# Exponentials of the memory slots brought to token order through a DRAM scratch instead of TensorE turnings

## The chip, the core and the metric

The kernel runs on one core of a Trainium2 chip. The metric is the device time of one execution in microseconds. Engines are named as in the profile: PE is TensorE (matmuls; PEld its weight loads), DVE is VectorE, ACT is ScalarE, POOL is GpSimd, SP is SyncE, whose queue issues most DMAs.

## The reference

An attention over 32 learned memory slots feeds a mixture of experts with one expert per token. All in float32.

```python
# attention: batch 8, heads 8, tokens S = 576, head size D = 64, slots M = 32
a = exp(phi - max over tokens); a = a / (sum over tokens + 1e-9)
k_m = einsum('bhsm,bhsd->bhmd', a, k); v_m = einsum('bhsm,bhsd->bhmd', a, v)
attn = softmax(q @ k_m^T / 8); x = attn @ v_m          # 576 tokens of 512 per batch
# experts: 8, hidden 1024
logits = normed(x) @ normed(expert_emb).T / tau; e = argmax(logits)
out = softmax(logits)[e] * (relu(x @ w1[e]) @ w2[e])
```

The part that the change touches is the first line: exp(phi - max), and the sums over tokens that use it as a weight.

## The kernel before

The eight batches run one after the other in a pipeline of three. While batch b goes through its expert, the attention of batch b + 1 (the object u in the code) is finished and its expert chosen, and the slots of batch m = b + 2 are made. The program is written out by hand in the order of each engine: every engine takes its instructions in that order. TensorE's work sets the steps. The first layer of a batch has 16 steps (first[0] to first[15]: two halves of 288 tokens by eight blocks of the hidden size, six matmuls each, L629); the second layer has 40 (second[0] to second[39]: the tail of 64 tokens in eight steps, L671, then tiles 0 to 3 of 128 tokens in eight steps each of three matmuls, L682). Each float32 product is made from three matmuls of split operands: the split of W2 into wh and wl is made by GpSimd (L599, L600), that of the hidden layer by ScalarE (hh, L632) and VectorE (hl, L635). The function steps() hangs the rest of the work on these steps.

The slots of a batch come as follows. load_phi reads phi, laid out with (4 heads x 32 slots) on the partitions and 576 tokens along a row, for two groups g of heads, into ex. largest (L413) takes the maximum over tokens on VectorE into nm, softmax (L428) the exponential on ScalarE, in place in ex. The sums over tokens are matmuls with tokens on the partitions, so ex has to be turned: turn (L450) makes nine 128 x 128 transposes on TensorE into te, and ScalarE copies them to eT (L451). slots (L470) multiplies eT with the keys and values kx and kl; blocks scales the result; flip turns it once more for the later steps. In a batch b of 1 or more, softmax of m stands at second[11] and second[14], turn at second[28], with the load of the next phi behind it, and slots at second[31], with load_kv of the next batch behind it. In batch 0 these stand at 18, 21, 32 and 35.

The attention of batch b + 1: its scores come out as sT, with heads and slots on the partitions; u.fill (L63) turns them by VectorE's 32 x 32 block transpose into x, with tokens on the partitions; there they are weighed and divided. u.lay (L99) writes x in 128-byte pieces to a DRAM scratch td, and three reads (L103, L105) bring it back to ea in token order. u.attend (L115) makes the rows po; VectorE reduces them to lg, the maximum m and the flags oh (L120, L122, L123); choose counts the tokens of each expert on TensorE (L156) and takes the largest to seli. SP reads seli, and issues the loads of W1 (w1s) and W2 (w2s) and two writes to DRAM (keep: ad and vd). In batch 0, whose steps lie later, fill is at second[3] and second[7], lay at second[7] and second[10], attend at second[24], [26] and [28], choose at second[29].

SP issues its DMAs in the order of the program; there are eight completion semaphores in turn, so each DMA also waits until the one eight places before it has landed. PSUM has four buffers m0 to m3 for sums (tag m) and four for the rest (tag t).

Of the kernel before, what the change touches and what calls it, by code (L numbers as in the profile page):

```python
# [8 lines left out]
F32 = mybir.dt.float32  # L9
# [10 lines left out]
P = 128  # L20
B, H, S, D, M = 8, 8, 576, 64, 32
N, DM, E, FF = B * S, H * D, 8, 1024
NG = 2
# [208 lines left out]
class Kernel:  # L232
# [4 lines left out]
    def __init__(self, ctx, tc, phiT, qT, kv, kvt, emb, tau, w1, w2, out):  # L237
        self.tc, self.nc = tc, tc.nc
        self.phiT, self.qT, self.kv, self.kvt, self.emb, self.tau = phiT, qT, kv, kvt, emb, tau
        self.w1 = w1.rearrange("e p (c f) -> e p c f", c=NC)  # L240
        self.w2 = w2.rearrange("e p (c f) -> e p c f", c=8)
        self.out = out
        self.st = ctx.enter_context(tc.tile_pool(name="st", bufs=1))
        self.wk = ctx.enter_context(tc.tile_pool(name="wk", bufs=2))
        self.ps = ctx.enter_context(tc.tile_pool(name="ps", bufs=1, space=PSUM))
        dp = ctx.enter_context(tc.tile_pool(name="dram", bufs=1, space=DRAM))
        st = self.st.tile
        self.ad = dp.tile([B, P, NG, S], F32, name="ad")
        self.vd = dp.tile([B, P, NC * D], F32, name="vd")
        self.td = dp.tile([B, S, NG, 4, 32], F32, name="td")  # L250

        self.ex = st([P, NG * S + 64], F32, name="ex")
        self.kx = [st([P, H, 2 * D], F32, name=f"kx{k}") for k in range(4)]
        self.kl = st([P, 4, 2 * D], F32, name="kl")
        self.qt = st([P, NC, S], F32, name="qt")
        self.eT = st([P, 9, P], F32, name="eT")
        self.kvb = st([P, 2, NG, 4, D], F32, name="kvb")
        self.kb, self.vb = self.kvb[:, 0], self.kvb[:, 1]
        self.kT = st([P, NC, D], F32, name="kT")
        self.sT = st([P, NG, S], F32, name="sT")  # L260

        self.vT = [st([P, NG, 2, D + 2 * E], F32, name=f"vT{i}") for i in range(2)]

        self.vv = st([P, NG, P + E], F32, name="vv")

        self.x = st([P, NG, BL, 32], F32, name="x")
        self.ea = st([P, NT, NG * P], F32, name="ea")
        self.rs, self.known = {}, set()
        self.aT = [st([P, NG, S], F32R, name=f"aT{k}") for k in range(2)]
        self.aw = st([P, NG, S2], F32, name="aw")  # L270

        self.w1s = st([P, NC, FF], F32, name="w1s")
        self.w2s = st([P, 8, DM], F32, name="w2s")
        self.wh = st([P, 8, DM], F32R, name="wh")
        self.wl = st([P, 8, DM], F32R, name="wl")
        self.gh = st([P, NG, FF], F32R, name="gh")
        self.gl = st([P, NG, FF], F32R, name="gl")
        self.hh = st([P, 8, S], F32R, name="hh")
        self.hl = st([P, 8, S], F32R, name="hl")
        self.h4 = st([P, 8, 64], F32, name="h4")  # L280

        self.gate = st([P, B, NT], F32, name="gate")
        self.idx = st([P, B, NT], F32, name="idx")
        self.fl = st([P, B, E], F32, name="fl")
        self.seli = st([1, B], I32, name="seli")
        self.halves = self.turns = 0
        self.tags, self.sums = 3, 0
# [72 lines left out]
    def load_phi(self, b, gs=range(NG)):  # L360
        if b < B:
            for g in gs:
                to = self.e(b, g)
                if g and b > 1:
                    self.nc.sync.dma_start(to[:, 64:], self.phiT[b, :, g, : 4 * P])
                    self.nc.sync.dma_start(to[:, :64], self.phiT[b, :, g, 4 * P :])
                else:
                    self.nc.sync.dma_start(to, self.phiT[b, :, g])

    def load_kv(self, b):  # L370
        if b < B:
# [38 lines left out]
        return self.rs[b]  # L410

    def largest(self, b, g):
        self.nc.vector.tensor_reduce(  # L413
            out=self.room(b)[0][:, g : g + 1], in_=self.e(b, g), axis=AX.X, op=ALU.max, negate=True
        )
        self.known.add((b, g))
# [28 lines left out]
    def turn(self, b, i0, i1):  # L445
        t = self.pt([P, 4, P], f"te{b}_{i0}")
        for i in range(i0, i1):
            g, k = divmod(i, 4)
            o = 5 * P * g + P * k if i < 8 else 4 * P
            self.nc.tensor.transpose(t[:, i - i0], self.ex[:, o : o + P], self.ident)  # L450
        self.nc.scalar.copy(self.eT[:, i0:i1], t[:, : i1 - i0])  # L451
        if i1 == 9 and b > 1:
            self.load_phi(b + 1)

    def slots(self, b, accs=None, gs=range(NG), ks=range(5), first=True, last=True):

        nc = self.nc
        if first:
            self.accs = accs or [self.pt([P, 2 * D], f"acc{b}_{g}") for g in range(NG)]
        accs = self.accs  # L460

        def to(i, g):
            r = slice(32 * i, 32 * i + 32)
            return accs[g][r, i] if len(accs[g].shape) == 3 else accs[g][r]

        def add(g, j, k):
            r = slice(64 * g, 64 * g + 64) if k == 4 else slice(P)
            e = self.eT[r, 4 * g + k if k < 4 else 8, 32 * j : 32 * j + 32]
            x = self.kl[r, j] if k == 4 else self.kx[k][:, 4 * g + j]
            nc.tensor.matmul(  # L470
                to(j ^ g, g), lhsT=e, rhs=x, start=first and k == ks[0], stop=last and k == ks[-1]
            )

        for g in gs:
            for k in ks:
                for j in range(4 if k < 4 else 0):
                    add(g, j, k)
        for j in range(4 if 4 in ks else 0):
            for g in gs:
                add(g, j, 4)  # L480
        if b > 1:
            self.load_kv(b + 1)

    def block(self, b, g, which=(0, 1), alone=False):

# [205 lines left out]
    def steps(self, b, t, u):  # L691


        first, second = ([[] for _ in range(n)] for n in (16, 40))
# [13 lines left out]
        if u:  # L708
            c, o = b + 1, 0 if b else 3
# [16 lines left out]
            o = 0 if b else 7  # L726
# [10 lines left out]
            second[32 + o].append(lambda: list(after))  # L737
            m = b + 2
            if m < B:
                for g in range(NG):  # L740
                    second[11 + 3 * g + o].append(lambda g=g: self.softmax(m, (g,)))
                second[18 + o].append(lambda: self.shares(m))
                second[(28 if b else 25) + o].append(lambda: [self.turn(m, i, min(i + 4, 9)) for i in (0, 4, 8)])
                at = second[(31 if b else 28) + o]
                at += [lambda: self.slots(m), lambda: self.blocks(m, 0), lambda: self.blocks(m, 1, True)]
                for g in range(NG):
                    second[(35 + 2 * g if b else 31 + g) + o].append(lambda g=g: self.flip(m, g))
# [281 lines left out]
```

## Time and profile before

| | us |
|---|---|
| median of 3 runs | 418.94 (418.16 to 420.54) |
| the profiled execution, its time | 419.85 |
| its span in the trace | 418.1 |
| PE busy | 404.8 |
| DVE busy | 262.0 |
| ACT busy | 169.6 |
| POOL busy | 173.0 |

The time of an execution holds the span and what lies around it. Batch 0's second layer begins at 49.5 us and batch 1's project step at 82.9 us; from batch 3 on a batch takes some 48.6 us. In the groups of the trace, a row has the line, the engine, the operation, out<-in by the program's names and the number of instructions. In the timeline a row has the start, the length, the engine and its line; what stands in brackets is the idle time of the engine before it and what ended that. Rows with SPq are the issues of DMAs, not their transfers. A row of windows has the stretch, its length, the busy time of PE, PEld, DVE, ACT and POOL with their instructions, the granted clock of TensorE (PEclk), the share of the 16 DMA engines and GB/s.

### The profile page before, as it was taken

The page shows a single profiled execution, that of the slowest core. Times are in us where ns is not written, and L with a number is a line of the kernel's source. Part 1 is how long each engine was busy: PE and PEld are TensorE (multiplying, and loading weights), DVE is VectorE, ACT ScalarE, POOL GpSimd, SP SyncE. Part 2 cuts the span into 40 slices and gives each one's busy share as a digit, 9 for nine tenths or more (in the row PEclk, how much of TensorE's full clock was granted, in tenths as well). Part 3 has the DMA queues.
Part 4 walks back from the last instruction along what each step waited for, and adds up shares of the span by engine and source line. Part 5 has one row for each costly group of instructions (what it writes and reads, how often), then busy time and mean ns, then how long its engine had stood idle before and what let it go on. Part 6 is the DMA issues. An engine that isn't in the chain of part 4 may idle for free. (4 is left out here: it accounts for less than half of the span.)

```text
span 418.1 us, 9433 instructions
## 1 busy us (share of the span) xinstructions
PE 404.8 (97%) x3491; PEld 328.7 (79%) x3491; DVE 262.0 (63%) x839; ACT 169.6 (41%) x468; POOL 173.0 (41%) x205
## 2 busy tenths in 40 slices
PE   7889999999999999999999999999999999999993
PEld 3458878788887978879887988879788888879783
DVE  5597894679664795549772795647955495745000
ACT  4475521465225722356313742347213661145110
POOL 0035671297032932168130960339331681359000
PEclk9999999999999999999999999999999999999997
DMA  8989934996679835994469916797349405690101
GB/s 266 348 308 375 364 72 117 313 362 251 153 229 396 320 57 126 361 368 192 76 216 390 386 53 143 253 380 314 63 132 355 159 0 98 204 402 2 38 36 47
DMA packets 69858, 91.19 MB, mean 218 GB/s; under 512 B 41800, under 2 KB 47688, under 8 KB 69808
## 3 DMA queue, kind: packets, MB, share of 16 engines
q1 hardware_dynamic: 66928, 82.00, 59.0%
q0 software_dynamic: 2688, 8.26, 5.3%
q8 instruction: 29, 0.48, 0.5%
q10 hardware_dynamic: 192, 0.28, 0.2%
q14 instruction: 21, 0.17, 0.1%
HBM read 71.19 MB, written 19.33 MB: 217 GB/s over the span
## 5 line engine op out<-in xcount | busy, mean ns | idle before, releaser
L629 PE MATMUL ph<-aT,gh 128*128 128x288 f32 x512 | 103.3, 297 | 0.5 <-DVE gl L613 0.5
L682 PE MATMUL py<-wh,hh 128*128 128x512 f32 x248 | 102.4, 413 | 0.0
L682 PE MATMUL py<-wl,hh 128*128 128x512 f32 x248 | 97.0, 391 | 0.3 <-POOL wl L600 0.3
L682 PE MATMUL py<-wh,hl 128*128 128x512 f32 x248 | 97.1, 392 | 0.0
L600 POOL TENSOR_TENSOR wl<-w2s,wh 128x512 fp32r<-128x512 f32 x64 | 83.9, 1311 | 5.2
L629 PEld LDWEIGHTS ph<-aT,gh 128*128 128x128 f32 x512 | 81.6, 188 | 3.1 <-DVE gl L613 1.4
L629 PE MATMUL ph<-aT,gl 128*128 128x288 f32 x256 | 75.3, 294 | 0.0
L635 DVE SCALAR_TENSOR_TENSOR hl<-ph,hh 128x288 fp32r<-128x288 f32 x128 | 56.1, 450 | 21.0 <-ACT hh L632 15.7
L687 ACT ACTIVATE ys<-py,gate 128x512 f32<-128x512 f32 (+1 forms) x39 | 25.1, 643 | 103.5 <-PE py L682 55.0
L632 ACT ACTIVATE hh<-ph 128x288 fp32r<-128x288 f32 x128 | 52.2, 416 | 32.6 <-PE ph L629 32.0
L793 POOL DMA_DIRECT2D out_dram<-ys x28 | 15.5, 553 | 117.3 <-ACT ys L687 109.6
L682 PEld LDWEIGHTS py<-wh,hh 128*128 128x128 f32 x248 | 46.6, 188 | 12.0 <-issue 4.3
L682 PEld LDWEIGHTS py<-wh,hl 128*128 128x128 f32 x248 | 46.5, 188 | 10.2
L682 PEld LDWEIGHTS py<-wl,hh 128*128 128x128 f32 x248 | 46.7, 188 | 8.5 <-POOL wl L600 0.7
L629 PEld LDWEIGHTS ph<-aT,gl 128*128 128x128 f32 x256 | 48.0, 188 | 0.0
L590 POOL TENSOR_TENSOR aT<-aw,aT 128x576 fp32r<-128x576 f32 (+3 forms) x20 | 23.7, 1205 | 47.0 <-PE py L682 33.8
L599 POOL CAST wh<-w2s 128x512 fp32r<-128x512 f32 x64 | 42.4, 663 | 0.7 <-DMA w2s<-w 0.6
L613 DVE TENSOR_TENSOR gl<-pg,gh 128x512 fp32r<-128x512 f32 x32 | 19.9, 683 | 34.8 <-ACT gh L612 34.8
L671 PE MATMUL py<-w2s,h 128*64 128x256 f32 x256 | 29.4, 382 | 0.0
L120 DVE TENSOR_REDUCE lg<-po 128x8 f32<-128x16 f32 x40 | 6.9, 174 | 31.7 <-PE po L115 30.4
L671 PEld LDWEIGHTS py<-w2s,h 128*64 128x64 f32 x256 | 17.7, 137 | 9.4 <-DVE hl L635 1.0
L115 PEld LDWEIGHTS po<-vv,aw 128*128 128x128 f32 x160 | 21.8, 189 | 3.2 <-ACT kT L517 1.0
(168 smaller groups left out, 506.7 us busy)
## 6 DMA issues: line engine op xcount, KB each, us to landing
kx<-kv SPq DMA_DIRECT2D x32, 512.0 KB, 7.1
w2s<-w SPq DMA_DIRECT2D x32, 512.0 KB, 10.7
w1s<-w SPq DMA_DIRECT2D x28, 512.0 KB, 6.6
out_dram<-ys POOLq DMA_DIRECT2D x28, 256.0 KB, 6.0
qt<-qT SPq DMA_DIRECT2D x12, 576.0 KB, 8.1
ad<-aw SPq DMA_DIRECT2D x8, 576.0 KB, 12.8
td<-x SPq DMA_DIRECT2D x56, 72.0 KB, 2.2
ea<-td SPq DMA_DIRECT2D x7, 512.0 KB, 4.2
```

The source lines that it names most:

```text
L115: nc.tensor.matmul(po[:, 144 * g : 144 * g + P + E], lhsT=k.aw[:, g, to], rhs=k.vv[:, g], start=True, stop=True)
L590: self.nc.gpsimd.tensor_tensor(out=al, in0=a, in1=ah.bitcast(F32), op=ALU.subtract)
L599: (copy or self.nc.scalar.copy)(h, x)
L600: self.nc.gpsimd.tensor_tensor(out=l, in0=x, in1=h.bitcast(F32), op=ALU.subtract)
L613: nc.vector.tensor_tensor(out=self.gl[:, g, f], in0=ps[g], in1=self.gh[:, g, f].bitcast(F32), op=ALU.subtract)
L629: nc.tensor.matmul(p, lhsT=w[:, g, fs], rhs=x[:, g, to], start=g == 0 and k == 0, stop=g == 1 and k == 2)
L632: nc.scalar.activation(self.hh[:, f, to], p, AF.Relu)
L635: nc.vector.scalar_tensor_tensor(out=self.hl[:, f, to], in0=p, scalar=0.0, in1=self.hh[:, f, to].bitcast(F32), op0=ALU.max, op1=ALU.subtract)
L671: nc.tensor.matmul(p[64 * j : 64 * j + 64], lhsT=self.h4[:, f], rhs=self.w2s[:, f, d * j : d * j + d], start=f == 0, stop=f == 7,)
L682: nc.tensor.matmul(p, lhsT=h[:, f, to], rhs=w[:, f], start=f == 0 and k == 0, stop=f == 7 and k == 2)
L687: nc.scalar.activation(y[:, :d], p, AF.Copy, scale=gate[:, i : i + 1])
L793: eng.dma_start(self.out[r : r + P], y)
```

## The change

From batch 2 on, TensorE's turn and ScalarE's copies are gone. In their place spread turns ex by VectorE's 32 x 32 transpose into a tile (sT for batch 2, x for later ones), send writes that tile in eight DMAs of 72 KB, in 128-byte pieces, to a new DRAM scratch pd, and gather reads pd back in four DMAs into eT in token order. Batches 0 and 1 still turn on TensorE.

This is done a batch ahead, so the maxima and exponentials move too. In a batch b of 1 or more, the end of the second layer makes the maxima (second[30]), exponentials (second[33]) and turnings (second[36], [37]) of batch m + 1, and at second[38] its writes and load_kv(m + 1); the next batch's first[12] gathers them, and first[13] loads the following phi. In batch 0 there is no batch ahead: second[11] to second[14] do maxima, exponentials, turnings and writes of batch 2, with the load of batch 3's phi ahead of the writes; second[22] gathers batch 2 and takes the maxima of batch 3, second[23] its exponentials, second[25] and [27] its turnings, second[32] its writes. load_phi no longer splits its second half in two.

```diff
     def load_phi(self, b, gs=range(NG)):
         if b < B:
             for g in gs:
-                to = self.e(b, g)
-                if g and b > 1:
-                    self.nc.sync.dma_start(to[:, 64:], self.phiT[b, :, g, : 4 * P])
-                    self.nc.sync.dma_start(to[:, :64], self.phiT[b, :, g, 4 * P :])
-                else:
-                    self.nc.sync.dma_start(to, self.phiT[b, :, g])
+                self.nc.sync.dma_start(self.e(b, g), self.phiT[b, :, g])
...
-        if i1 == 9 and b > 1:
-            self.load_phi(b + 1)
+    def tiles(self, b, g):
+        return self.x[:, g] if b > 2 else self.sT[:, g].rearrange("p (n m) -> p n m", m=32)
+    def spread(self, b, g):
+        if b < B:
+            self.nc.vector.transpose(self.tiles(b, g), self.e(b, g))
+    def send(self, b):
+        for g in range(NG if b < B else 0):
+            for l in range(4):
+                r = slice(32 * l, 32 * l + 32)
+                self.nc.sync.dma_start(self.pd[b, :, g, l].rearrange("(n t) m -> t n m", t=32), self.tiles(b, g)[r])
+    def gather(self, b):
+        nc = self.nc
+        for g in range(NG):
+            pd = self.pd[b, :, g].rearrange("s l m -> s (l m)")
+            nc.sync.dma_start(self.eT[:, 4 * g : 4 * g + 4], pd[: 4 * P].rearrange("(i p) x -> p i x", p=P))
+            nc.sync.dma_start(self.eT[64 * g : 64 * g + 64, 8], pd[4 * P :])
...
-        if b > 1:
-            self.load_kv(b + 1)
...
+                if b:
+                    first[12].append(lambda: self.gather(m))
+                    first[13].append(lambda: self.load_phi(m + 1))
+                else:
...
+                    second[14] += [lambda: self.load_phi(m + 1), lambda: self.send(m)]
+                    second[22].append(lambda: self.gather(m))
                 for g in range(NG):
-                    second[11 + 3 * g + o].append(lambda g=g: self.softmax(m, (g,)))
+                    second[30 if b else 22].append(lambda g=g: self.largest(m + 1, g))
...
-                second[(28 if b else 25) + o].append(lambda: [self.turn(m, i, min(i + 4, 9)) for i in (0, 4, 8)])
```

On VectorE in batch 0's second layer, from the last division of batch 1's attention to the shares of batch 2, stood before (nm is batch 2's maxima, po, lg, m and oh are the routing of batch 1, rs the sums of batch 2):

```order
L93 STREAM_TRANSPOSE aw<-x 128x64
L413 TENSOR_REDUCE nm_930<-ex 128x1 x2
L120 TENSOR_REDUCE lg_490<-po_0_959 128x8
L120 TENSOR_REDUCE lg_490<-po_1_962 128x8
L122 TENSOR_REDUCE m_492<-lg_490 128x2
L123 TENSOR_TENSOR oh_493<-lg_490,m_492 128x16
L439 TENSOR_SCALAR rs_932<-sm_931 128x1
L439 TENSOR_SCALAR rs_932<-sm_931 32x1 x4
L443 RECIPROCAL rs_932<-rs_932 128x2
```

At the same place of the same engine there is now this (nm_905 is batch 2's maxima, nm_965 batch 3's, which read ex once batch 3's phi is in it):

```order
L93 STREAM_TRANSPOSE aw<-x 128x64
L411 TENSOR_REDUCE nm_905<-ex 128x1 x2
L458 STREAM_TRANSPOSE sT<-ex 128x576 x2
L411 TENSOR_REDUCE nm_965<-ex 128x1 x2
L120 TENSOR_REDUCE lg_490<-po_0_982 128x8
L120 TENSOR_REDUCE lg_490<-po_1_985 128x8
L122 TENSOR_REDUCE m_492<-lg_490 128x2
L123 TENSOR_TENSOR oh_493<-lg_490,m_492 128x16
L458 STREAM_TRANSPOSE x<-ex 128x576
L437 TENSOR_SCALAR rs_907<-sm_906 128x1
L437 TENSOR_SCALAR rs_907<-sm_906 32x1 x4
L441 RECIPROCAL rs_907<-rs_907 128x2
```

Two turnings of batch 2 and the maxima of batch 3 now stand ahead of the routing of tiles 0 and 1, and a turning of batch 3 behind it; the second turning of batch 3 stands in the same way between the routing of tiles 2 and 3 and that of tile 4.

On SP in batch 0's second layer stood, from the writes of batch 1's attention to the loads of its expert (td and ea the attention in token order, seli the expert chosen):

```order
L99 DMA td<-x 32x18x32 x8
L103 DMA ea<-td 128x4x256
L105 DMA ea<-td 64x256 x2
L170 TENSOR_LOAD seli
L170 ISA x2
```

There is now, at the same place (ex is batch 3's phi, pd the new scratch with batch 2's exponentials):

```order
L99 DMA td<-x 32x18x32 x8
L103 DMA ea<-td 128x4x256
L105 DMA ea<-td 64x256 x2
L364 DMA ex<-phiT 128x576 x2
L465 DMA pd<-sT 32x18x32 x8
L472 DMA eT<-pd 128x4x128
L473 DMA eT<-pd 64x128
L472 DMA eT<-pd 128x4x128
L473 DMA eT<-pd 64x128
L170 TENSOR_LOAD seli
L170 ISA x2
```

The load of phi, the eight writes and the four reads stand between the ea reads and the reading of the chosen expert. From batch 1's loads of W2 on, into batch 2's first layer, SP's order is now the following (vd is the second keep write):

```order
L600 DMA vd<-vT_81 512x1x64
L465 DMA pd<-x 32x18x32 x8
L370 DMA kl<-kvt 64x512 x2
L372 DMA kx_71<-kv 128x1024
L372 DMA kx_72<-kv 128x1024
L372 DMA kx_73<-kv 128x1024
L372 DMA kx_74<-kv 128x1024
L382 DMA qt<-qT 128x1152 x2
L472 DMA eT<-pd 128x4x128
L473 DMA eT<-pd 64x128
L472 DMA eT<-pd 128x4x128
L473 DMA eT<-pd 64x128
```

Where phi stood behind vd before, there are now the eight writes; the gather and the next phi follow q, ahead of the td writes of the next routing.

More of the change, by code (lines that the diff above doesn't have):

```diff
@@ L250, in __init__ @@
         self.td = dp.tile([B, S, NG, 4, 32], F32, name="td")
+        self.pd = dp.tile([B, S, NG, 4, 32], F32, name="pd")
         self.ex = st([P, NG * S + 64], F32, name="ex")
@@ L412, in largest @@
     def largest(self, b, g):
+        if b >= B:
+            return
         self.nc.vector.tensor_reduce(
@@ L739, in steps @@
             if m < B:
-                for g in range(NG):
-                    second[11 + 3 * g + o].append(lambda g=g: self.softmax(m, (g,)))
+                if b:
+                    first[12].append(lambda: self.gather(m))
+                    first[13].append(lambda: self.load_phi(m + 1))
+                else:
+                    for g in range(NG):
+                        second[11].append(lambda g=g: self.softmax(m, (g,)))
+                        second[13 + g].append(lambda g=g: self.spread(m, g))
+                    second[14] += [lambda: self.load_phi(m + 1), lambda: self.send(m)]
+                    second[22].append(lambda: self.gather(m))
+                for g in range(NG):
+                    second[30 if b else 22].append(lambda g=g: self.largest(m + 1, g))
+                    second[33 if b else 23].append(lambda g=g: self.softmax(m + 1, (g,)))
+                    second[36 + g if b else 25 + 2 * g].append(lambda g=g: self.spread(m + 1, g))
+                second[38 if b else 32].append(lambda: self.send(m + 1))
+                second[38 + (not b)].append(lambda: self.load_kv(m + 1))
                 second[18 + o].append(lambda: self.shares(m))
-                second[(28 if b else 25) + o].append(lambda: [self.turn(m, i, min(i + 4, 9)) for i in (0, 4, 8)])
                 at = second[(31 if b else 28) + o]
```

## The prediction

> **What bounds the kernel now.** I read the page's first part, then TensorE's waits, then the timeline of each engine around the removed work, because an average over 418 us says nothing of one place.
>
> ```profile
> span 418.1 us, 9433 instructions
> PE 404.8 (97%) x3491; PEld 328.7 (79%) x3491; DVE 262.0 (63%) x839; ACT 169.6 (41%) x468; POOL 173.0 (41%) x205
> ```
>
> TensorE is busy for 404.8 of 418.1 us, VectorE for 63%. TensorE's own waits, longest total first (total, times, longest):
>
> ```profile
> PE acc0t L470 <- DMA kx<-kv: 1.1, 2, 0.6
> ...
> PE py L682 <- POOL wl L600: 0.3, 1, 0.3
> ```
>
> There are ten rows, and none is above 1.1 us. So TensorE's queue of instructions is the time: what leaves it is gained in full, and whatever makes it stand is lost in full. The profiled execution took 419.85 us, 0.9 us above the median of 418.94; I sum changes against the profile and add the sum to the median. A difference of about 0.5% (2.1 us) is what a measurement of this kernel can tell from no change.
>
> **What is removed from TensorE.** TensorE's timeline around one set of turnings (start, length), and the group of all sets behind batch 1:
>
> ```profile
> 73.12 0.39 PE L682 MATMUL py<-wl,hh 128*128 128x512 f32 x1
> 73.35 0.40 PE L682 MATMUL py<-wh,hl 128*128 128x512 f32 x1
> 73.59 1.15 PE L450 MATMUL te<-ident,ex 128*128 128x128 f32 x9
> 74.49 0.48 PE L682 MATMUL py<-wh,hh 128*128 128x512 f32 x1
> 74.81 0.40 PE L682 MATMUL py<-wl,hh 128*128 128x512 f32 x1
> L450 PE MATMUL te<-ident,ex x54: 272/273/273, 73.6 to 314.8; 128*128 128x128 f32 x54
> ```
>
> The matmuls of L682 start 0.23 us apart (73.12 to 73.35). From 73.35 to 74.81 stand 1.46 us, in which two such steps, 0.46, would have passed: a set costs 1.00 us, not the 9 x 0.273 = 2.5 us that its durations add up to, since matmuls overlap. 54 turnings are six sets (batches 2 to 7): 6 x 1.00 = **6.0 us off the path**. The eighteen copies to eT leave ScalarE, which is off the path (41%).
>
> **What is added in batch 0.** Here the change is not the same as in later batches. All of it happens within one pass of the second layer, and a load stands on the chain. VectorE and ScalarE in that stretch of before:
>
> ```profile
> 61.43 1.37 DVE L413 TENSOR_REDUCE nm<-ex 128x1 f32<-128x576 f32 x2
> 66.15 0.17 DVE L120 TENSOR_REDUCE lg<-po 128x8 f32<-128x16 f32 x1 [3.36 <-PE po L115]
> ...
> 67.03 0.17 DVE L123 TENSOR_TENSOR oh<-lg,m 128x16 bf16<-128x16 f32 x1
> 67.12 0.78 DVE L439 TENSOR_SCALAR rs<-sm 128x1 f32<-128x1 f32 x5
> 67.94 0.17 DVE L443 RECIPROCAL rs<-rs 128x2 f32<-128x2 f32 x1
> ...
> 71.16 0.17 DVE L123 TENSOR_TENSOR oh<-lg,m 128x8 bf16<-128x8 f32 x1
> 62.95 0.76 ACT L428 ACTIVATE ex<-ex,nm 128x576 f32<-128x576 f32 x1
> 63.62 0.19 ACT L428 ACTIVATION_READ_ACCUMULATOR ex<-ex,nm 128x1 f32 x1
> L63 DVE STREAM_TRANSPOSE x<-sT x14: 760/767/772, 50.6 to 340.5; 128x576 f32<-128x576 f32 x14
> ```
>
> The first two turnings (batch 2's exponentials into sT) cost nothing: they start when ScalarE's exponentials are out (63.62 + 0.19 = 63.81 for the second) and the last ends at about 64.6, inside the 3.36 us in which VectorE waits anyway. But the next row of VectorE is then the maximum of batch 3, which reads ex as load_phi(3) leaves it. VectorE takes its rows in order, so the routing of batch 1 (lg, m, oh) stands behind that load. When does it land? SP's issues in before:
>
> ```profile
> 57.59 5.50 SPq L99 DMA_DIRECT2D td<-x  x8
> 65.36 0.39 SPq L103 DMA_DIRECT2D ea<-td  x1
> 65.79 1.33 SPq L105 DMA_DIRECT2D ea<-td  x2
> 72.78 1.98 SPq L398 DMA_DIRECT2D w1s<-w  x4
> ```
>
> The load's two halves come behind the ea reads, so their issue begins at 65.79 + 1.33 = 67.12. At about half an us each both are out by 68.1. The time from issue to landing of those ea reads and of the four w1s loads of this batch, and two stretches, with their share of the DMA engines and GB/s at the end:
>
> ```profile
> DMA to landing us min/median/max: 4.2/4.4/4.7
> DMA to landing us min/median/max: 4.1/6.4/7.8
> 58.00:64.00 6.00, 5.68 (x25) 4.35 (x25) 4.59 (x10) 2.32 (x5) 2.52 (x4) 1.00 0.82 157
> 222.00:228.00 6.00, 6.00 (x45) 4.93 (x31) 2.42 (x10) 2.65 (x9) 0.00 (x0) 1.00 1.02 412
> ```
>
> The last ea read, out at 66.5, lands at 70.7 to 71.2. The load's 576 KB follow in the same queue; at 412 GB/s they take 1.4 us: landed at about 72.1. That is my value. The early end is the shortest of the w1s landings, 4.1 us for 512 KB, taken down to 2.4 us for a half of 288 KB: 70.5. The late end gives the second half 5.4 us, between the longest ea read and the median w1s load: 73.5. The trace speaks for a queue in order. The Trainium skill (DMA: Bandwidth & Descriptors, Anatomy of one DMA) gives a fit of 2.0 us and bytes over 436 GB/s for one DMA alone, on GpSimd's path. By that estimate a half is in 2.7 us behind 68.1, at 70.8, and the sum below is 1.3 us lower; the ea rows, at 4.2 us and more for 512 KB, are slower than it.
>
> From 72.1 VectorE has, before oh of tile 4 is out: the second maximum 0.69 (half of 1.37); lg, lg, m, oh without their wait, some 0.7; a turning into x, 0.70 net; the five sums and the reciprocal, 1.0 (67.12 to 68.11); lg, lg, m, oh again, 0.7; a second turning, 0.70; lg, m, oh, 0.55. Together 5.05 us, so oh of tile 4 comes at 77.15. And TensorE:
>
> ```profile
> 71.26 0.18 PE L156 MATMUL po<-eb,ones 128*128 128x8 bf16 x1
> 71.30 0.27 PE L156 MATMUL po<-oh,ones 128*128 128x8 bf16 x5
> 76.75 1.95 PE L470 MATMUL acc<-kx,eT 128*32 128x128 f32 x64
> 82.86 1.52 PE L610 MATMUL pg<-w1s,vT 64*32 64x512 f32 x24
> ```
>
> The counting matmuls L156 need oh and ran at 71.30 right behind it (71.16 + 0.17). They stand in the middle of tile 2's L682, which queue behind them. So TensorE **stands from 71.3 to 77.15: 5.85 us** (4.2 by the early end, 7.3 by the late).
>
> The stop has a second price. The clock in two stretches at the end of before (TensorE's last matmul lies in the first; PEclk is the third from the end), and the warming matmuls at the start of the kernel (x, least, median and longest ns, first and last start):
>
> ```profile
> 410.09:413.50 3.41, 1.39 (x12) 1.19 (x10) 0.48 (x1) 0.00 (x0) 0.00 (x0) 1.00 0.25 77
> 413.50:416.91 3.41, 0.00 (x0) 0.00 (x0) 0.00 (x0) 0.00 (x0) 0.00 (x0) 0.50 0.03 7
> L352 PE MATMUL hot<-ones x7: 554/634/634, 1.0 to 3.6; 128*128 128x512 bf16 x7
> L352 PE MATMUL hot<-ones x5: 379/379/554, 3.6 to 4.6; 128*128 128x512 bf16 x5
> ```
>
> After 3.41 us of which TensorE worked 1.39, the clock was halved. At the start seven matmuls from 1.0 to 3.6 came 0.43 us apart, the next five to 4.6 some 0.25, so nearly 3 us of work brought the clock up. A stop of 5.85 us holds a mostly idle 3.41 us wherever such stretches begin, so I take the clock as halved until one busy stretch has passed: 1.7 to 5.1 us at half speed, a loss of 0.9 to 2.6, **1.7 us** as middle. The Trainium skill (TensorE: Matmul & The Clock Gate, What's actually happening) asks for a whole idle window of about 3.4 us. By it a stop of 5.85 would lose the clock in some 7 cases of 10, 1.2 us on average; the row, where 41% of work did not keep the clock, decides.
>
> What comes late next? The choice of the expert, and so the w1s issue on SP, moves by the same 5.85 us, and the sums from the count on are alike: w1s lands 7.8 us or less after an issue that ends at 74.76, against 82.86 where it is needed. Batch 0's set, gone, makes that need 1.0 us earlier, and the gather of 576 KB goes ahead of w1s. That would cost up to 1 us, but the lost clock leaves more time than that: nothing taken. The pd writes of 576 KB follow the load of phi at 157 GB/s (stretch 58 to 64, the same 128-byte writes), 3.8 us to 5: in by 77.5. The gather then lands by 81, and the matmuls that read eT (76.75 before) come at 77.15 + 5.45 - 1.0 = 81.6. Nothing taken; up to 1 us if the writes are slower.
>
> **What is added in batches 1 to 5.** Maxima, exponentials and turnings move to the end of the second layer, 1.4, 1.9 and 1.4 us on engines with gaps there. SP issues eight writes behind W2, then kv and q, and the gather and the next phi behind those. Who could wait is VectorE's fill of x (L63), since the writes read x, and behind it hl, whose PSUM TensorE needs:
>
> ```profile
> 230.29 3.08 SPq L376 DMA_DIRECT2D kx<-kv  x4
> 249.00 4.91 SPq L99 DMA_DIRECT2D td<-x  x8
> 184.60 0.46 DVE L635 SCALAR_TENSOR_TENSOR hl<-ph,hh 128x288 fp32r<-128x288 f32 x1 [0.30 <-ACT hh L632]
> 185.39 0.46 DVE L635 SCALAR_TENSOR_TENSOR hl<-ph,hh 128x288 fp32r<-128x288 f32 x1 [0.33 <-ACT hh L632]
> 238.59 0.77 DVE L63 STREAM_TRANSPOSE x<-sT 128x576 f32<-128x576 f32 x1
> ```
>
> The kx issue waits for W2's last piece by its queue slot, so W2 is in at 230.3. Two keep writes (704 KB, 1.7 us) and the pd writes (3.8 us) follow: all in at 236 to 237, the half that this fill needs about 2 us sooner, against 237.6 (238.59 less the 1.0 gained). Nothing taken; below, a rival. Kv, q, gather and phi then move 4.7 MB, 11.5 us at 412 GB/s: done by 248.5, as the td writes of the next routing are issued (249.0), and long before eT is read. So the DMA queue is full but not late; an ea read that comes a us later has slack before VectorE's norm. w1s and W2 stand ahead of all that is added and are not touched.
>
> **Sum:** -6.0 + 5.85 + 1.7 = **+1.55 us**: 419.85 to 421.4 in a profile, 418.94 to **420.5** as a time. Nearly the whole gain is given back in one place.
>
> **Rivals.** *Nearly the whole gain stays* (0.13): the load of phi lands by 69 and the clock holds. Then TensorE stands 2.8 us at most, -6.0 + 2.8 = -3.2: 415.7, less if sooner. For it: the engines moved only 157 GB/s in the stretch before. Against it: the ea reads, 4.2 us and more. *Slower: the fill of x waits in every batch* (0.12). The place is L63 behind the pd writes. TensorE has four PSUM buffers in the first layer and fills one in 0.79 us (hl at 184.60 and 185.39), so about 2.4 us of delay are free; it decides if the writes land past 240, 5 us after my estimate for the first half. Each us beyond costs five times: with 1 us, +5 on top of +1.55, 425.5. For it: the writes are 128-byte pieces at 157 GB/s, and DMA share is 1.02 just before. Against: two us of margin and the buffers. *Slower within the forecast's mechanism:* load at 73.5, clock lost for 5.1 us: -6.0 + 7.3 + 2.6 = +3.9: 422.8.
>
> **Chances.** The forecast's mechanism has 0.75; its sums run from -1.8 (early load, clock kept) to +3.9, 417.1 to 422.8. Above +2.1 lies a bit over a third of that, 0.28, and 0.47 lies within 2.1. With the rivals: faster 0.13, same 0.47, slower 0.40. The range of eight in ten leaves out most of the fast rival and the worst of the slow one: 416.5 to 424.5.
>
> **What would show it.** In the profile after: no te in batches 2 to 7; the six places at 0.23 us steps. In batch 0, VectorE's maximum waits 6 to 8 us for DMA ex, and TensorE's L156 waits 5 to 7 us for oh; PEclk falls to 0.5 for some us behind 75. No wait of VectorE's fill for pd in later batches, whose length is 1.0 us less than before. I am wrong if L156 waits under 3 us, if PEclk stays at 1.0, or if another TensorE wait above 1 us recurs per batch.

## The result and the profile after

| | median | least to most | runs |
|---|---|---|---|
| before | 418.66 us | 418.06 to 420.54 | 16 |
| after | 421.19 us | 419.97 to 422.66 | 16 |

The ratio of after to before is 1.0059 (95% interval 1.0044 to 1.0073): the kernel is 2.5 us slower, by the interval 1.8 to 3.1. I had forecast 420.5, 1.55 us slower. The page of the profiled execution after (busy times, TensorE's granted clock in 40 slices, and the DMA queue of the loads with its packets, MB and share):

```profile
span 420.7 us, 9413 instructions
...
PE 400.9 (95%) x3437; PEld 324.6 (77%) x3437; DVE 270.1 (64%) x851; ACT 161.9 (38%) x450; POOL 173.1 (41%) x205
...
PEclk9999999699999999999999999999999999999998
...
q1 hardware_dynamic: 101776, 89.08, 68.4%
```

TensorE has 54 matmuls less and is busy for 3.9 us less, yet the span is 2.6 us longer. The clock, which held before, falls in one slice, the eighth (73.6 to 84.1 us). TensorE's waits, the longest three of twelve:

```profile
PE po L156 <- DVE lg L120: 6.4, 1, 6.4
PE hot L353 <- DVE ones L292: 1.0, 1, 1.0
PE pg L628 <- DMA w1s<-w: 0.8, 1, 0.8
```

One long wait is new, it occurs once, and it is a little longer than all that was to be gained (6.4 us against 6.0). VectorE's timeline shows what it waits for; each row's last bracket is the idle time before it and what ended it:

```profile
63.44 1.54 DVE L458 STREAM_TRANSPOSE sT<-ex 128x576 f32<-128x576 f32 x2 [0.28 <-ACT ex L426]
73.04 1.43 DVE L411 TENSOR_REDUCE nm<-ex 128x1 f32<-128x576 f32 x2 [8.06 <-DMA ex<-phiT]
74.39 0.25 DVE L120 TENSOR_REDUCE lg<-po 128x8 f32<-128x16 f32 x2
...
75.05 0.78 DVE L458 STREAM_TRANSPOSE x<-ex 128x576 f32<-128x576 f32 x1
...
77.26 0.78 DVE L458 STREAM_TRANSPOSE x<-ex 128x576 f32<-128x576 f32 x1
...
78.33 0.17 DVE L123 TENSOR_TENSOR oh<-lg,m 128x8 bf16<-128x8 f32 x1
```

VectorE has nothing to do for 8.06 us: the maxima of batch 3 stand first in its order and wait for phi. The routing of batch 1 (lg to oh) comes behind them, though the matmuls that make its rows po ran from 65.8 to 71.1. TensorE over the same time:

```profile
71.36 0.40 PE L700 MATMUL py<-wh,hl 128*128 128x512 f32 x1
78.15 0.17 PE L156 MATMUL po<-eb,ones 128*128 128x8 bf16 x1 [6.40 <-DVE lg L120]
...
78.58 0.78 PE L700 MATMUL py<-wh,hh 128*128 128x512 f32 x1
79.15 0.63 PE L700 MATMUL py<-wl,hh 128*128 128x512 f32 x1
79.58 0.63 PE L700 MATMUL py<-wh,hl 128*128 128x512 f32 x1
...
90.83 1.95 PE L628 MATMUL pg<-w1s,vT 64*32 64x512 f32 x32
```

The next matmul was due 0.23 us behind 71.36, at 71.59; it came at 78.15, 6.56 us later. Behind the stop the steps of L700 are 0.43 us apart (79.15 to 79.58) instead of 0.23. Four stretches of 3.41 us with the clock in the third column from the end:

```profile
72.32:75.73 3.41, 0.00 (x0) 0.00 (x0) 2.62 (x7) 1.62 (x4) 0.00 (x0) 1.00 0.98 180
75.74:79.15 3.41, 0.87 (x7) 0.71 (x7) 2.89 (x18) 0.00 (x0) 0.00 (x0) 0.50 0.65 149
79.15:82.56 3.41, 3.41 (x9) 2.65 (x8) 3.27 (x17) 0.69 (x1) 2.89 (x3) 0.50 0.63 166
82.56:85.97 3.41, 3.41 (x58) 2.75 (x59) 0.86 (x5) 0.00 (x0) 0.56 (x1) 1.00 0.95 318
```

A stretch with no matmul is followed by 6.8 us at half clock, in which TensorE worked from 78.15 on, for 4.4 us.

The length of a batch is read from the starts of its projection (pg, the first matmuls of a batch). Before, two of them in the steady part:

```profile
131.46 1.53 PE L610 MATMUL pg<-w1s,vT 64*32 64x512 f32 x24
180.07 1.52 PE L610 MATMUL pg<-w1s,vT 64*32 64x512 f32 x23
```

and after:

```profile
138.40 1.09 PE L628 MATMUL pg<-w1s,vT 64*32 64x512 f32 x16
185.99 1.09 PE L628 MATMUL pg<-w1s,vT 64*32 64x512 f32 x16
```

48.61 us before, 47.59 after. With all such starts the account of the two profiles is this:

| | start of batch 0 | batch 0 | batch 1 | batches 2 to 5, each | batch 6 |
|---|---|---|---|---|---|
| before | 28.0 | 54.85 | 48.60 | 48.61 | 44.16 |
| after | 28.4 | 62.46 | 47.58 | 47.59 | 44.16 |

Five batches are 1.02 us shorter, 5.1 in all; batch 0 is 7.6 longer. That is its own set of turnings (-1.0), the stop (+6.56), and what is left, 2.05, which I put down to the clock (4.4 us at half speed can lose 2.2; hold, below, measures it apart).

### The profile page after: what moved, and what is told of

It is laid out like the page before. It is cut to its first block, busy times and chain, and to the rows that moved or that the text cites. A ratio compares the mean times of both kernels' runs of the same rounds, so it can differ in the third digit from the quotient of the medians.

```text
span 420.7 us, 9413 instructions
## 1 busy us (share of the span) xinstructions
PE 400.9 (95%) x3437; PEld 324.6 (77%) x3437; DVE 270.1 (64%) x851; ACT 161.9 (38%) x450; POOL 173.1 (41%) x205
## 5 line engine op out<-in xcount | busy, mean ns | idle before, releaser
L700 PE MATMUL py<-wh,hh 128*128 128x512 f32 x248 | 102.6, 414 | 0.0
L700 PE MATMUL py<-wl,hh 128*128 128x512 f32 x248 | 97.7, 394 | 0.3 <-POOL wl L618 0.3
L700 PE MATMUL py<-wh,hl 128*128 128x512 f32 x248 | 97.6, 394 | 0.0
L700 PEld LDWEIGHTS py<-wh,hh 128*128 128x128 f32 x248 | 47.1, 190 | 12.6 <-issue 4.5
L700 PEld LDWEIGHTS py<-wh,hl 128*128 128x128 f32 x248 | 47.0, 189 | 10.3
L700 PEld LDWEIGHTS py<-wl,hh 128*128 128x128 f32 x248 | 47.1, 190 | 8.8 <-POOL wl L618 0.7
```

The lines of the kernel that those rows point to most:

```text
L700: nc.tensor.matmul(p, lhsT=h[:, f, to], rhs=w[:, f], start=f == 0 and k == 0, stop=f == 7 and k == 2)
```

## The experiments

Theory A, on which the prediction stands: in one place of batch 0 VectorE's order puts batch 1's routing behind a load; the stop that follows and the clock behind it give back what six sets of turnings bring. Theory B: the scratch's traffic and the moved steps cost in every batch. All ratios are to runs of the kernel before on the same chip; batch lengths are read as above. They come from one execution each, which took from 1.05 us less (phifirst) to 1.9 us more (late3) than its kernel's median, so they say where time went and not how much a kernel takes.

| kernel | median us | ratio (interval) | batch 0 | batch 1 | later, each |
|---|---|---|---|---|---|
| late3 | 419.03 | 1.0006 (0.9988 to 1.0024) | 60.42 | 49.04 | 47.59 |
| hold | 420.47 | 1.0033 (1.0017 to 1.0049) | 60.88 | 49.09 | 47.59 |
| phifirst | 418.87 | 0.9995 (0.9982 to 1.0009) | 56.43 | 50.14 | 47.59 |
| keep2 | 414.76 | 0.9893 (0.9868 to 0.9919) | 54.42 | 49.20 | 47.59 |
| early2 | 414.91 | 0.9907 (0.9885 to 0.9929) | 53.93 | 51.19 | 47.59 |
| early3 | 415.11 | 0.9910 (0.9895 to 0.9925) | 54.50 | 49.26 | 47.59 |
| cover | 415.41 | 0.9907 (0.9884 to 0.9929) | 54.72 | 49.84 | 47.59 |
| early5 | 415.60 | 0.9927 (0.9912 to 0.9942) | 54.38 | 49.13 | 47.59 |
| keep3 | 415.44 | 0.9926 (0.9911 to 0.9941) | 54.42 | 49.41 | 47.59 |
| early4 | 421.45 | 1.0049 (1.0032 to 1.0067) | 54.20 | 56.16 | 47.59 |
| early6 | 420.45 | 1.0046 (1.0027 to 1.0065) | 57.48 | 51.31 | 47.59 |
| double | 432.48 | 1.0317 (1.0298 to 1.0336) | 61.75 | 52.72 | 47.78 to 52.56 |

### The stop taken away: late3

```diff
-                    second[30 if b else 22].append(lambda g=g: self.largest(m + 1, g))
-                    second[33 if b else 23].append(lambda g=g: self.softmax(m + 1, (g,)))
-                    second[36 + g if b else 25 + 2 * g].append(lambda g=g: self.spread(m + 1, g))
-                second[38 if b else 32].append(lambda: self.send(m + 1))
+                    second[30 if b else 33].append(lambda g=g: self.largest(m + 1, g))
+                    second[33 if b else 35].append(lambda g=g: self.softmax(m + 1, (g,)))
+                    second[36 + g if b else 37 + g].append(lambda g=g: self.spread(m + 1, g))
+                second[38 if b else 39].append(lambda: self.send(m + 1))
```

> In batch 0 the maxima, exponentials and turnings of batch 3 go behind the choice of batch 1's expert (places 33, 35, 37, 38, 39 of the second layer), so VectorE's routing no longer stands behind load_phi(3). Theory A (the stop at the counting matmuls comes from that one place): the 6.4 us wait of L156 for VectorE is gone. Naively that gives 421.2 - 6.6 - 2.0 = 412.6. But SP still issues the gather of batch 2 (75.6 to 78.2, behind the pd writes) ahead of the value load and w1s, so a second stop should appear a little later: the slots' matmuls want eT at about 76 and have it at about 80.5, 4.7 us, with about 1.7 us of clock: 418.7 - 6.0 + 4.7 + 1.7 = 419.1, between 418 and 421. Theory B (the added traffic and steps cost in every batch, batch 0 is no special place): 421, no new wait in batch 0, and the distances of later batches not 1.0 us shorter.

The wait of L156 is gone, and the next late thing takes its place, TensorE's wait for the gather:

```profile
75.17 0.39 PE L700 MATMUL py<-wh,hl 128*128 128x512 f32 x1
79.43 3.64 PE L490 MATMUL acc<-kx,eT 128*32 128x128 f32 x64 [3.88 <-DMA eT<-pd]
```

The slots' matmuls were due at 75.4 and came at 79.43: 4.0 us. Here too the clock goes, though the stretch ahead of it was not quite empty:

```profile
75.05:78.46 3.41, 0.51 (x3) 0.08 (x1) 1.92 (x8) 1.63 (x4) 0.61 (x2) 1.00 0.73 194
78.46:81.87 3.41, 2.44 (x48) 2.47 (x52) 0.00 (x0) 0.00 (x0) 0.00 (x0) 0.50 0.71 204
```

419.03, as expected with the gather next late; the naive 412.6 is excluded. Theory B is wrong in all it said: batch 0 did change, and later batches are 1.02 us shorter.

### The clock alone: hold

```diff
+        self.warm(28, hot=self.pt([P, 512], "hold"))
...
+            if not b:
+                second[29].append(self.hold)
```

> The changed kernel with 28 idle bf16 matmuls (about 0.21 us each, 6 us) on TensorE ahead of the counting matmuls of batch 0, where it stood for 6.4 us. They compute nothing that is used. Theory A (the stop cost its length plus a halved clock behind it): the clock stays at 1.0 behind 75 us and the time falls by the 2.0 us that were lost at half speed: 419.2. Rival (the clock record is not what slowed the steps, or the stop alone costs): 421.2, the same.

```profile
70.65 6.22 PE L353 MATMUL hold<-ones 128*128 128x512 bf16 x28
77.44 0.17 PE L156 MATMUL po<-eb,ones 128*128 128x8 bf16 x1 [0.57 <-DVE lg L120]
...
78.19 0.39 PE L705 MATMUL py<-wl,hh 128*128 128x512 f32 x1
78.42 0.40 PE L705 MATMUL py<-wh,hl 128*128 128x512 f32 x1
```

TensorE still cannot go on until 77.44, but behind the idle work the steps are 0.23 apart at once, and batch 0 is 1.6 us shorter than after's with a stop 0.2 us longer: about 1.8 us was the clock. Only a part of it shows in the time (0.7 us by the medians, 1.1 by the ratios, whose intervals overlap a little): batch 1 is 1.5 us longer than after's 47.58, because its projection now begins before w1s is in. So the half clock had hidden a late load. The prediction said "the lost clock leaves more time than that"; this is that sentence, tested.

### The load earlier: phifirst

SP's order becomes td, phi(3), ea, pd instead of td, ea, phi(3), pd.

```diff
+        if b > 1:
+            self.back()
+
+    def back(self):
...
         td = k.td[b].rearrange("s g l m -> s (g l m)")
...
-                    second[14] += [lambda: self.load_phi(m + 1), lambda: self.send(m)]
+                    second[14] += [lambda: self.load_phi(m + 1), u.back, lambda: self.send(m)]
```

> The changed kernel with load_phi(3) issued ahead of the three ea reads in batch 0 instead of behind them: SP waits there for the td writes until 65.2 anyway, and ex is free from 65.0. Theory A (the stop's length is the landing of that load plus 5.3 us of VectorE): phi lands at about 69.5 instead of 73, the stop of L156 falls from 6.4 us to 3 or 4, and the time by as much: 418. If a stop of that length keeps the clock, 416. Rival (the load lands late because of the pd writes and the ea reads beside it, whatever the order): the stop stays at 5.5 us or more and the time at 421.

VectorE's maxima are now apart, one for each half of the load, which was issued from 63.31 to 64.42:

```profile
66.22 0.75 DVE L417 TENSOR_REDUCE nm<-ex 128x1 f32<-128x576 f32 x1 [2.18 <-DMA ex<-phiT]
68.42 0.75 DVE L417 TENSOR_REDUCE nm<-ex 128x1 f32<-128x576 f32 x1 [1.45 <-DMA ex<-phiT]
...
73.00 0.17 DVE L129 TENSOR_TENSOR oh<-lg,m 128x8 bf16<-128x8 f32 x1
```

```profile
72.82 0.17 PE L162 MATMUL po<-eb,ones 128*128 128x8 bf16 x1 [1.96 <-DVE lg L126]
```

The second half is in 4.0 us behind the end of its issue, and oh is out 4.75 us behind the start of the second maximum (68.42 to 73.17), just as in the changed kernel (its second maximum starts at about 73.75, oh ends at 78.50). So the landing of that load sets the length of the stop, 1.96 us here. This stop kept the clock at 1.00 throughout. That was luck in part: it lay across two of the 3.41 us stretches in which the clock record changes, which held 2.32 and 2.42 us of matmuls (68.54 to 71.95 and on to 75.37). The last section shows how little a stretch may hold. The time is 418.87 and not 416, since batch 1 gives back 2.55 us at its projection, which waits for w1s. (This profiled execution took 417.82, 1.05 below the kernel's median; its batches 0 to 5 together come out 1.0 us shorter than before's, the median not at all.)

### All gained, nothing stopped: keep2 and early2

Both make batch 2's exponentials at the start of batch 0's second layer and take batch 3's steps late, as late3. keep2 turns batch 2 on TensorE there; early2 sends it through the scratch, turned into w1s, which is free then. keep2 reads the last rows of batch 2's phi where the changed layout no longer has them, which changes that part of the computation and not the work: its output is not the reference's, and its time is that of a probe.

```diff
+                        first[12].append(lambda g=g: self.largest(m, g))
+                        second[0].append(lambda g=g: self.softmax(m, (g,)))
...
+                    second[4] += [lambda i=i: self.turn(m, i, min(i + 4, 9)) for i in (0, 4, 8)]
+                    second[4].append(lambda: self.load_phi(m + 1))
```

early2 has in place of the last two lines `second[4].append(lambda g=g: self.spread(m, g))` and `second[5].append(lambda: self.send(m))`, with the gather ahead of the ea reads and phi behind them.

> Batch 2's exponentials are made at the start of batch 0's second layer and turned by TensorE as before (nine matmuls), load_phi(3) follows at once, while the DMA engines idle; batches 3 to 7 go through the scratch as in the change, batch 3's steps late in batch 0. Theory A: five sets gone at 1.0 us and no stop: 418.7 - 5.0 = 413.7. Theory B (scratch traffic and moved steps cost in the later batches): 418 or more.

> All of the change, but batch 2's maxima, exponentials and turnings come 10 us earlier in batch 0 (maxima in the first layer, turnings into w1s, which is free there, at step 4 of the second), its writes are issued at step 5, its gather ahead of the ea reads, load_phi(3) behind them, and batch 3's steps late as in later batches. Theory A: all six sets gained and nothing given back: 418.7 - 6.0 = 412.7, no wait of TensorE above 1.1 us. Rival (the trip of batch 2 costs wherever it stands in batch 0, by VectorE's later fill or by later ea reads): a new wait of TensorE in batch 0 above 1 us, 414 to 418.

Both beat the kernel before by 0.9 to 1.1%, and so the changed one too, with no stop at the counting matmuls and a clock that holds. But early2 gives 3.9 us and not 6. Batches 2 to 5 have their 1.02 each, batch 0 has 0.92, and batch 1 is 3.6 us too long (in an execution of 416.46 us, 1.55 above the median, so the typical loss may be smaller). TensorE's timeline at its start:

```profile
81.02 1.06 PE L632 MATMUL pg<-w1s,vT 64*32 64x512 f32 x8
83.41 1.05 PE L632 MATMUL pg<-w1s,vT 64*32 64x512 f32 x4 [1.32 <-DMA w1s<-w]
84.68 1.48 PE L632 MATMUL pg<-w1s,vT 64*32 64x512 f32 x18 [0.23 <-DMA w1s<-w]
```

The projection comes by pieces, as w1s lands. It was issued from 72.36, behind the ea reads and phi.

### Why the rest does not come: early3, early4, cover, early5, early6, keep3

early3 issues phi(3) at place 4 of the second layer instead. early4 is early3 with a small write that reads w1s between the loads of w1s and W2, so that W2 starts when w1s is in. cover is early3 with 7 idle bf16 matmuls at place 34.

```diff
-        if b == 1:
-            k.load_phi(3)
...
+                    second[4].append(lambda: self.load_phi(m + 1))
                     second[5].append(lambda: self.send(m))
```

```diff
+        self.nc.sync.dma_start(self.wd, self.w1s[:1, :, :1])
+        self.load_w2(e)
```

> As early2, but load_phi(3) goes ahead of batch 2's writes (about 54 us, where the DMA engines idle) instead of behind the ea reads (70.4). In early2 the expert's weights of batch 1 (w1s) were issued at 72.4, 2.1 us behind the choice, landed up to 10.5 us after issue and TensorE's projection lost 3.6 us. Theory A (that loss is SP's order and the load in front of w1s): w1s is issued at about 71 and lands by 82.5, the loss falls to 1.6 us as in keep2, time 413. Rival (w1s is late because W2 shares the engines with it): the loss stays, 415.

> As early3, and in batch 0 a write of four numbers that reads w1s stands between the w1s and the W2 loads on SP's queue, so that W2 of batch 1 starts only when w1s has landed. Theory (w1s would land in time if it had the engines to itself): no wait of the projection, batch 1 as long as the later ones (47.6), 411.5. Rival (its own issue and landing time is the limit): the loss of 1.6 us stays, 413; or W2, now 4 us later, is waited for in batch 1: 414 or more.

> early3 with seven idle bf16 matmuls (7 x 0.213 = 1.5 us, computing nothing that is used) on TensorE in batch 0 between the choice of the expert and the projection of batch 1, where batch 0's set of turnings stood before the change. Theory A (early3's batch 1 is 1.7 us too long because the projection waits for w1s, about 10.5 us behind the start of its issue, and the turnings were part of the cover): the added work is free, time as early3, 415.1, batch 0 1.5 us longer and batch 1 as much shorter. Rival (the loss has another cause): 416.6.

early3's batch 1 loses 1.67 us instead of 3.6, as expected, but its time was to be 413 and its median is no better than early2's (the intervals overlap). So how much phi ahead of w1s cost is not shown. In early4 w1s had the engines to itself and the loss stayed (81.86 its start, the pieces until 84.8): W2 is not what delays w1s. What came instead is the rival of the prediction, the fill that waits for the pd writes, since W2 and all behind it on SP were 10 us later:

```profile
DVE x L63 <- DMA pd<-x: 4.9, 1, 4.9
DVE ea L142 <- DMA ea<-td: 2.5, 1, 2.5
DVE nm L419 <- DMA ex<-phiT: 2.4, 2, 1.3
```

TensorE stood 4.1 us for hl behind that fill and the clock went. cover came out 0.3 us above early3 with an interval 1.9 us wide, and its batches did not move by 1.5 us as the theory had it. In early3 TensorE waits for kvb ahead of the projection (0.48 and 0.43 us, from 78.5 to 80.0); in cover that wait is gone, so the idle work may have taken its place. As a test of w1s it settles nothing.

early5 makes the choice of the expert two places earlier and has GpSimd issue the gather; early6 has SP issue the gather and GpSimd the ea reads. keep3 is keep2 with batch 2's phi laid out as before and the choice four places earlier.

```diff
-            second[22 + o] += [lambda: self.load_w2(u.choose()), self.parts, lambda: self.keep(c)]
+            second[22 + o if b else 27] += [lambda: self.load_w2(u.choose()), self.parts, lambda: self.keep(c)]
```

(25 in keep3; the routing's places move along.)

> As early3, with the choice of batch 1's expert two places (1.4 us) earlier in batch 0 (its routing at places 24, 25, 26, the count at 27, the sums behind it at 28) and batch 2's gather issued by GpSimd, idle from 65 to 70.7, instead of SP, so that SP has only the ea reads ahead of w1s. Theory A (the w1s load must be issued 10.5 us before the projection, which starts at 81.5): w1s is issued at 69.2 instead of 71.9, no wait is left, batch 1 is 47.6 us long, time 415.1 - 1.7 = 413.4. Rival (the ea reads and the gather crowd w1s wherever they stand): the loss stays, 415; or the counting matmuls wait for VectorE up to 1 us: 414.5.

> As early5 (choice of batch 1's expert two places earlier), but now the gather of batch 2 is on SP again, where it fills the time until the choice, and batch 1's ea reads, which wait for the td writes until about 70, are issued by GpSimd. In early5 SP stood at those reads until 71.7 although the expert was chosen at 69.0, and w1s was issued at 72.6. Theory A (w1s has to be issued about 10.5 us before the projection at 81.5, and SP's order kept it): w1s is issued at 69.4, no wait of the projection, batch 1 is 47.6 us long, time 415.1 - 1.6 = 413.5. Rival (w1s lands late because the engines are full in that stretch): it still lands at about 83 and the time stays at 415.

> keep2 (batch 2 turned by TensorE early in batch 0, batches 3 to 7 through the scratch), with phi of batch 2 laid out for those turnings as in the kernel before, and with the choice of batch 1's expert earlier: routing at places 22, 23, 24, the count at 25, the sums at 26. In keep2 VectorE waited 3.2 us for the first routing matmuls and SP was free from 68.3 to 72.2, so here nothing stands in front of w1s. Theory A (the projection waits for w1s, about 10.5 us behind the start of its issue): w1s is issued at about 69.4, batch 1 is 47.6 us long instead of 49.2, batches 0 and 1 take 102.1 us together (before: 103.45), time 414.8 - 1.6 = 413.2. Rival (w1s lands at 83 whenever it is issued, or the counting matmuls now wait): 414.8 or more.

All three missed, each for a reason of its own. In early5 the expert was chosen at 69.0, and SP stood at the ea reads, which wait for td, so that w1s was issued at 72.56 as ever. In early6 the ea reads by GpSimd landed later, VectorE waited 4.95 us for them until 78.39, and the copies to kvb and TensorE's flips came behind it (its profile also has the clock halved for one stretch from 28.41 us, where TensorE had stood 2.00 us for batch 0's w1s; the other profiles don't. That can be up to 1.7 us of its batch 0, half of the 3.30 us that TensorE worked there. The edit hands batch 0's ea reads to GpSimd too; whether that made w1s late wasn't tried). keep3 is the clean case: w1s was issued at 69.76 and the projection ran at 81.51 in one piece of 32 matmuls, without a wait. So w1s lands in time if it is issued early enough, as theory A said. Then VectorE was next late. TensorE's wait, and VectorE's rows ahead of the one that ended it:

```profile
86.31 0.53 PE L652 MATMUL ph<-aT,gh 128*128 128x288 f32 x2 [1.76 <-DVE gl L636]
```

```profile
82.07 0.78 DVE L463 STREAM_TRANSPOSE x<-ex 128x576 f32<-128x576 f32 x1
82.77 0.66 DVE L217 TENSOR_TENSOR eq<-oh,rev 128x40 f32<-128x40 bf16 x1
...
83.70 1.06 DVE L219 TENSOR_SCALAR idx<-m 128x5 f32<-128x5 f32 x1
...
85.57 2.48 DVE L636 TENSOR_TENSOR gl<-pg,gh 128x512 fp32r<-128x512 f32 x4
```

The turnings of batch 3 (0.78 each) and the gates of batch 1 stand ahead of gl, and some of the gates take far longer than elsewhere (L219, see the last section). That these rows made gl late is read from their order; no run moved them. In every version without the stop the end of batch 0 gives back 1.5 to 1.8 us or more, through w1s or through VectorE. A version with the full 6 us was not found.

### How near the steady batches are to a limit: double

```diff
+        for g, pd in [(g, pd) for pd in (self.pd, self.pe)[: 2 if b > 2 else 1] for g in range(NG if b < B else 0)]:
```

> The changed kernel, but batches 3 to 7 issue their eight pd writes twice, the second eight into a scratch that nothing reads: 576 KB and about 9 to 12 us of SP's issue more in each of five batches. It shows how near the steady batches are to the point from which the writes cost. Theory A (queue full but not late, margins of 2 us at the fill of x and 2.4 us of PSUM buffers): the doubled writes are past the margin, waits of VectorE's fill for pd appear in every batch, 2 to 6 us each, and the batches are 1 to 6 us longer: 426 to 450. Rival (the writes are far from any limit): no change, 421.

```profile
DVE x L63 <- DMA pe<-x: 12.6, 5, 4.2
```

```profile
PE ph L648 <- DVE hl L654: 8.6, 4, 3.4
```

Five waits of the fill for the doubled writes, four of which reach TensorE: 13.6 us against before, 11.3 against the changed kernel. The eight added writes took 4.4 to 5 us of SP's issue a time (99.19 to 103.63 for the first), not the 9 to 12 that were expected. Of that the fill felt 2.5 us on average, from 0.74 to 4.2, TensorE 3.4 at most, and the clock went with some of it: up to 5.1 us a batch. The writes as they are cost nothing, but by the difference, an estimate, the spare time ahead of the fill runs from some 3.7 us down to 0.3.

## Why the prediction was right

- **The bound.** TensorE's queue was the time: each set taken out brought 1.02 us per batch (forecast 1.00 from start distances, not the 2.5 of added durations).
- **The stop.** Place, waiting engine and cause as forecast: VectorE's maximum for phi (8.06 us, just past the forecast 6 to 8), L156 for oh (6.4, within 5 to 7). Its size was 6.56 us against 5.85. The mis-sized term is the landing of phi, taken at 72.1; the first maximum began at 73.04 and the second near 73.75. What moved it was the issue: the ea reads took 2.66 us on SP instead of 1.33, so phi was issued from 68.33 and not 67.12:

```profile
65.62 2.66 SPq L105 DMA_DIRECT2D ea<-td  x2
68.33 1.07 SPq L364 DMA_DIRECT2D ex<-phiT  x2
69.45 6.01 SPq L465 DMA_DIRECT2D pd<-sT  x8
```

  From the end of its issue to the second maximum were 4.35 us, near phifirst's 4.0. VectorE's chain from there, taken at 5.05, measured 4.75. Why the same reads took twice as long to issue stays open; no run was made for it. It is no accident of one execution: late3 and hold have 2.80 and 2.73, phifirst 2.10, while keep2, keep3, early2, early3 and early5, which turn batch 2 earlier, have 1.15 to 1.24.
- **The clock.** Lost, as forecast, with 4.4 us of work at half speed (forecast 1.7 to 5.1); 2.05 us by the account, about 1.8 by hold, 1.7 in the sum.
- **w1s and gather, "nothing taken".** Right for this kernel, for the reason given: the stop and the half clock covered them. late3, hold, phifirst and early2 show 1.5 to 4 us there as soon as the cover is gone. As a forecast of what a mended kernel gains, the "up to 1 us" was too small: it let w1s land within 7.8 us of the end of its issue, and in keep2, keep3 and early2 to early5 the last piece landed 8.7 to 10.5 us behind its own issue.
- **Batches 1 to 5, nothing.** Right: 47.59 each, no wait of the fill in the profile after. The rival's mechanism is real (early4, double) and was not reached, though by double's figures one batch had only some 0.3 us to spare, where the prediction had two us and the buffers.
- **Sum.** -6.1 + 6.56 + 2.05 = +2.5 against +1.55. It closes because 2.05 is the remainder; with hold's 1.8 it gives +2.3. The time lies in the range, but above the +2.1 from which the prediction spoke of slower: to that it gave 0.40, to the same 0.47. The fast rival's condition (phi by 69, clock kept) is what phifirst made, and there the next late load ate the gain: 418.87 instead of 415.7.

## What to carry to other kernels

A prefetch that runs a batch ahead in the steady state needs a start: look at the first batch by itself, where all that the others get a batch early has to fit into one pass, and at whose work stands behind its wait in the engine's order. Before pricing the removal of a stop, list what is next late behind it (here the gather, w1s, VectorE's rows ahead of gl), since a stop hides every load that is late by less. Here a stop that left too little work in one 3.41 us stretch of the clock cost a further 2 us. Idle matmuls in the stop (6 us of them) saved that, but the time fell by about half of it, since the slow stretch had hidden a late load.

## What the runs showed of the hardware

- The clock record changes at 75.74 and 82.56 in the changed kernel and at 78.46 and 85.28 in late3: two stretches of 3.41 us each time. In late3 a stretch with 0.51 us of matmuls in 3.41 still lost it; phifirst's stop of 2 us did not. The Trainium skill (TensorE: Matmul & The Clock Gate, What's actually happening) speaks of an idle window of about 3.4 us; the length agrees, but the window need not be wholly idle. The traces of all fourteen kernels here, behind their first 7 us and cut into such stretches at the places where the record changes, show how much work was too little: each of the 21 stretches at whose end the clock fell to half held 1.52 us of matmuls or less, and each that kept it at 1.00 held 1.70 or more. Both nearest cases are in early6:

```profile
24.98:28.39 3.41, 1.52 (x35) 0.51 (x25) 3.27 (x7) 1.94 (x6) 0.88 (x2) 1.00 1.05 398
28.39:31.80 3.41, 3.30 (x23) 1.67 (x24) 1.45 (x5) 1.31 (x4) 0.00 (x0) 0.50 1.02 400
89.85:93.26 3.41, 1.70 (x44) 1.15 (x39) 3.24 (x10) 1.93 (x4) 3.33 (x4) 1.00 0.70 155
```

  So in these traces the border lay between 1.52 and 1.70 us of matmuls in 3.41, and where a stop falls counts as well as its length. By this, an estimate, phifirst's stop of 1.96 us would have lost the clock, narrowly, if it had lain within one stretch: that leaves 1.45 us.
- w1s, 2 MB in four loads, takes long to come even with little queued behind it: in early4 it was issued from 72.15, and the write that reads it went out at 83.56, 11.4 us later. From the first issue to the last landing keep3 had 10.3 us, phifirst 8.5 and early2 12.2.
- In keep3 a VectorE row on 128x5 elements took 1.06 us, against a mean of 171 ns for that line in the changed kernel. The row ended at 84.76; a GpSimd row (wl from w2s and wh) ran from 83.46 to 84.74. The Trainium skill (SBUF — State Buffer, Who interferes with whom) describes a pair of ports that VectorE and GpSimd hold by turns for a whole instruction; the two ends agree with that, though no run here took the GpSimd work away.
- The eight pd writes took 4.45 us of SP's issue with idle DMA engines (early2, from 53.97) and 6 to 12.7 where the engines were busy.
